# Attention with a gated convolution behind it: two narrow score blocks at a chunk's end are given one relu and one square in common

## The chip, the cores and the metric

One Trainium2 chip, of which one core is used. TensorE (PE in the profile) multiplies, VectorE (DVE) and ScalarE (ACT) work elementwise, GpSimd (POOL) does a little, and SyncE (SP) issues the transfers. The metric is the time of one launch on the device, in microseconds (us), as a median of several runs.

## The reference

For each of 8 batches of 3,200 rows, with `z` of 64 columns and `u`, `v` of 256:

```
scores = (1/3200) * z @ z.T               # 3200 x 3200
attn   = max(scores, 0) ** 2
x      = u * (attn @ v)
gate   = sigmoid(causal convolution of x, 5 taps, a weight per column and tap)
out    = ((x @ w_val) * gate) @ w_out
```

All is float32. The kernel reaches that precision by splitting a factor into a high and a low part, `hi = round(a)` and `lo = a - hi`, and by adding three products: low times high, high times low and high times high.

## The kernel before

The 3,200 keys of a batch are 25 tiles of 128 rows: 12 pairs of tiles and one single tile, 13 *blocks*. The queries are cut into 6 chunks of 4 tiles (512 columns), numbered 0 to 5, and one single tile that is done with chunk 5. A *step* is one block of keys for one chunk of queries, and a chunk runs through its 13 blocks at the *places* 0 to 12.

For a step TensorE first makes the scores `s` of the block (`scores`, L464), three steps ahead of use (`AHEAD`, L68). Then `weights_of` (L600) turns them into weights: on ScalarE a relu out of the accumulator banks into `a` (L643), a square in place (L644) and a copy to the high part `ah` (L646); on VectorE `al = a - ah` (L652). The attention `acc` (`attend`, L718) then multiplies `v`'s parts with `ah` and `al`. Its first product reads `ah`, its second `al`. TensorE runs two multiplications of 64 rows side by side, and each step's attention is in two parts, whose row halves change sides. The second part of a step waits in a list (`left`) until other work for TensorE comes up; that is mostly the scores of the step three ahead, which part the two parts of one step.

The scores are symmetric. What a chunk has computed is turned by VectorE (L518, L528), written to `mir` in memory by SP's queue and fetched as `m` by a later chunk (`mirrored`, L282), which then has no scores to compute there.

Two steps of a chunk are narrow. The single tile (`SINGLE`) has 512 scores for each row in place of 1,024. The second of the chunk's own two pairs (`own(c, 1)`) computes one half of its scores, 512 again, and takes the other from `m` (`halves`, L506; L608 to L628, with the relu at L611, the square at L612, and the two copies at L621). It is moved to the chunk's last place, L298. In the chunks in which no fetched block comes between, the single tile is at place 11 and this pair at place 12.

The work of the chunk behind (convolution, gate, the multiplication by `w_val`) is set out over the steps by tables (`BEHIND`, L328): at place 8 VectorE makes the second half of `gv` (`gate_value`, L912), at place 9 ScalarE copies it to `gvh` (`gate_value_high`, L916). In the loop over the steps (L1499) the order within a step is: TensorE's attention and scores, then the table's work (L1573), then `weights_of` for the step three ahead (L1579). Each engine takes its instructions in the order in which they are written.

The scores go to two bank pairs, `s0` and `s1`, in turn (`s_bank`, L455); each is 2 x 512 columns wide, and a narrow step uses 2 x 256 of it.

Of the kernel before, what the change touches and what calls it, by code (L numbers as in the profile page):

```python
# [7 lines left out]
F32 = mybir.dt.float32  # L8
# [4 lines left out]
P = 128  # L13
# [4 lines left out]
def attn_glu_kernel(  # L18
# [430 lines left out]

    st_, at = {}, {}  # L450

    next_s = [0]
    held_s = [None]

# [9 lines left out]
    def scores(b, c, i, terms=range(3)):  # L464
        if not terms:
            return
        k, n = tiles(c, i)
        w = sizes[c] * P
        if (b, c, i) not in st_:
            st_[b, c, i] = s_bank()  # L470
        s = st_[b, c, i]

        q = zt[b, c][:, :, :w].rearrange("p x (t a r) -> p x a t r", t=sizes[c], r=BLK)
        if has_copy(b, c, i):
            q = zq[b, c][:, :, :w].rearrange("p x (a y) -> p x a y", a=P // BLK)
        if halves(b, c, i):
            q, w = q[:, :, :, 2 * BLK :] if has_copy(b, c, i) else q[:, :, :, 2:], w // 2
        a = P // BLK
        sides = []
        for j in range(2):  # L480
            g, t = homes[k + (0 if n == 1 else j)]
            ks = slice(t * P, (t + 1) * P)
            qs = slice(j * (a // 2), (j + 1) * (a // 2)) if n == 1 else slice(0, a)
            kk = zt[b, g]
            mms = []
            for m in terms:
                kp, qp = (((0, 0), (0, 1), (1, 0)) if b == c == i == 0 else ((0, 1), (1, 0), (0, 0)))[m]
                mms.append((s[:, j, : w // 2 if n == 1 else w], kk[:, kp, ks], q[:, qp, qs], m == 0, m == 2))
            if both(c, i):
                for m in terms:  # L490
                    kp, qp = ((0, 1), (1, 0), (0, 0))[m]
                    q1 = zt[b, ONE][:, qp, j * (P // 2) : (j + 1) * (P // 2)]
                    mms.append((s[:, j, w // 2 : w // 2 + P // 2], kk[:, kp, ks], q1, m == 0, m == 2))
            sides.append(mms)
        side_by_side(*sides)
# [92 lines left out]
    def second_block(a, hi, lo, s):  # L588
        each = a.shape[1] // 2
        for j in range(2):  # L590
# [6 lines left out]
                v_low(0, 1)  # L597
            rest(lo[:, x], a[:, x], hi[:, x])

    def weights_of(b, c, i):  # L600

        k, n = tiles(c, i)
        w = sizes[c] * P
        ah = sb.tile([P, 2 * CW], F32R, name="ah", bufs=AHEAD + 1)
        al = sb.tile([P, 2 * CW], F32R, name="al", bufs=AHEAD + 1)
        cols = columns(c, i)
        hi, lo = ah[:, :cols], al[:, :cols]
        if halves(b, c, i):  # L608
            s = st_.pop((b, c, i))
            a = sb.tile([P, 2 * CW], F32, name="a", bufs=2)[:, :w]  # L610
            nc.scalar.activation(a.rearrange("p (j x) -> p j x", j=2), s[:, :, : w // 2], AF.Relu, scale=scale)  # L611
            nc.scalar.activation(a, a, AF.Square)  # L612
            m = m_in.pop((b, c, i))[:, :w]
            m = m.rearrange("p (a j x) -> p a j x", a=P // BLK, j=2)

            his, los = (x.rearrange("p (j a h x) -> p a j h x", j=2, a=P // BLK, h=2) for x in (hi, lo))
            a = a.rearrange("p (j a x) -> p j a x", j=2, a=P // BLK)
            parts = [(m, his[:, :, :, 0], los[:, :, :, 0])]
            parts.append((a, *(x[:, :, :, 1].rearrange("p a j x -> p j a x") for x in (his, los))))
            for src, h, _ in parts:  # L620
                nc.scalar.copy(h, src)  # L621
            at[b, c, i] = (ah, al)

            def rests():
                for src, h, l in parts:
                    nc.vector.tensor_tensor(l, src, f32(h), op=ALU.subtract)  # L626

            return rests  # L628
        if mirrored(b, c, i):
            a = m_in.pop((b, c, i))[:, :cols].rearrange("p (a j x) -> p a j x", a=P // BLK, j=n)  # L630
            hi, lo = (x.rearrange("p (j a x) -> p a j x", a=P // BLK, j=n) for x in (hi, lo))
        else:
            s = st_.pop((b, c, i))
            a = sb.tile([P, 2 * CW], F32, name="a", bufs=2)[:, :cols]
            each = n * w // 2
            if both(c, i):
                to = a[:, n * w :].rearrange("p (j x) -> p j x", j=2)
                nc.scalar.activation(to, s[:, :, each : each + P // 2], AF.Relu, scale=scale)
            if b == c == 0 and i < 2:
                at[b, c, i] = (ah, al)  # L640
                first_block(a, hi, lo, s) if i == 0 else second_block(a, hi, lo, s)
                return lambda: None
            nc.scalar.activation(a[:, : n * w].rearrange("p (j x) -> p j x", j=2), s[:, :, :each], AF.Relu, scale=scale)  # L643
            nc.scalar.activation(a, a, AF.Square)  # L644
        if cast_on_scalar(b, c, i):
            nc.scalar.copy(hi, a)  # L646
        else:
            nc.vector.tensor_copy(hi, a)
        at[b, c, i] = (ah, al)

        def rest():
            nc.vector.tensor_tensor(lo, a, f32(hi), op=ALU.subtract)  # L652
            if (b, c, i) == (0, 0, 2):
                v_high(b, 3)
                v_low(b, 3)
            if not mirrored(b, c, i):
                if c == 1 and two_pairs(b, c) and i == own(c, 0) and place[b, c, i] == 0:
                    return lambda: turn(b, c, i, a)
                turn(b, c, i, a)

        return rest
# [823 lines left out]
    with tc.manual_schedule():  # L1485
# [13 lines left out]
        for s in range(min(todo), END + 1):  # L1499
# [3 lines left out]
            late = steps[AHEAD - 1] if s == 0 else None  # L1503
            places, ends = (value_places(b, cm), project_places(b, cm)) if s >= 0 else ((), ())
            piece = PIECES[len(places)][places.index(p)] if p in places else None
            terms = [] if lacks(s) or not ahead else list(range(3))
            if s in FILL:
                no_wait(zeros[:, :P], zeros, "misc1", FILL[s])
            k = b * n_chunks + cm if s >= 0 else 0
# [4 lines left out]
            if s >= WHOLE_FROM:  # L1514
                assert not left and not terms and not piece and not before
                if s < END:
                    for h in range(DH):
                        attend_whole(b, c, i, h)
                        if s == WHOLE_FROM and h == 0:
                            one_turn(len(GROUPS) - 1)  # L1520
            else:
                fill, whole, bare = [], False, before and ends and not terms
                if before and ends:
                    project(*before, 0)
                    scores(*ahead, terms)
                    terms, fill = [], [(project, *before, 1, 0, len(ends) + 1)]
                elif before:
                    project(*before, 0)
                    scores(*ahead, terms[:1])
                    project(*before, 1)  # L1530
                    terms = terms[1:]
                if p in ends:
                    fill = [(project, *divmod(k - 2, n_chunks), 1, 1 + ends.index(p), len(ends) + 1)]
                if piece:
                    fill = [(value, *behind, *piece)]
                    behind = None
                fill += filling.get(s, [])
                if s >= NP and p == 0 and (bare or not before):

                    scores(*ahead, terms)  # L1540
                    for h in range(DH):
                        attend_whole(b, c, i, h)
                    terms, whole = (), True
                elif s >= 0 and c != ONE:
                    attend(b, c, i, 0)
                if late:
                    scores(*late)
                    attend(b, c, i, 1)
                    whole = True
                if s == -AHEAD:  # L1550
                    scores(*ahead, terms)
                    z_turn(0, 1)
                    terms = []
                if behind:
                    value(*behind, 0)
                if terms:
                    scores(*ahead, terms)
                for fn, *args in fill:
                    fn(*args)
                if s >= 0 and not whole and c != ONE:  # L1560
                    left.append((b, c, i))
                if terms or fill or behind or s + 1 == WHOLE_FROM:
                    for n in range(len(left)):
                        attend(*left.pop(0), 1, again=n > 0)
                if behind:
                    value(*behind, 1)
# [8 lines left out]
            keep()  # L1575
            if late:
                held.append(weights_of(*late))
            if ahead:
                held.append(weights_of(*ahead))  # L1579
                if s < 0 or s != ends_main[b, cm][1] - 1:  # L1580
                    for do in held[:]:
                        held.remove(do)
# [111 lines left out]
```

## Time and profile before

| | |
|---|---|
| median of 3 runs | 2251.35 us (2249.55 to 2252.07) |
| span of the profiled execution, first to last instruction | 2248.5 us |
| TensorE busy | 2241.3 us |
| VectorE busy | 1851.4 us |
| ScalarE busy | 1700.3 us |
| TensorE's granted clock over the span | 1.000 |

The profile is of one execution, and its own time is known by its span alone, 2.85 us under the median. Busy time is the union of an engine's instructions. Multiplications are pipelined and their ends are modelled, so one is judged by its start and by the start of the next. A row of a timeline that joins several instructions shows the first start, the whole stretch and the count.

### The profile page before, as it was taken

The page shows a single profiled execution, that of the slowest core. Times are in us where ns is not written, and L with a number is a line of the kernel's source. Part 1 is how long each engine was busy: PE and PEld are TensorE (multiplying, and loading weights), DVE is VectorE, ACT ScalarE, POOL GpSimd, SP SyncE. Part 2 cuts the span into 40 slices and gives each one's busy share as a digit, 9 for nine tenths or more (in the row PEclk, how much of TensorE's full clock was granted, in tenths as well). Part 3 has the DMA queues.
Part 4 walks back from the last instruction along what each step waited for, and adds up shares of the span by engine and source line. Part 5 has one row for each costly group of instructions (what it writes and reads, how often), then busy time and mean ns, then how long its engine had stood idle before and what let it go on. Part 6 is the DMA issues. An engine that isn't in the chain of part 4 may idle for free.

```text
span 2248.5 us, 49885 instructions
## 1 busy us (share of the span) xinstructions
PE 2241.3 (100%) x20235; PEld 1881.1 (84%) x20235; DVE 1851.4 (82%) x2284; ACT 1700.3 (76%) x2136; POOL 93.4 (4%) x134
## 2 busy tenths in 40 slices
PE   9999999999999999999999999999999999999999
PEld 7888888888888988888888898888888889888888
DVE  8888788877889778887888968888788887888777
ACT  8986688766887668876698766987669776697764
POOL 0200000000000000000000000000000000000001
PEclk9999999999999999999999999999999999999999
DMA  6558867888677886788677876778867778687663
GB/s 156 115 140 206 211 147 163 189 184 196 159 169 180 187 195 153 175 188 195 170 172 166 191 192 166 171 180 181 209 142 186 178 181 203 144 187 175 169 177 103
DMA packets 702423, 390.79 MB, mean 174 GB/s; under 512 B 410608, under 2 KB 635888, under 8 KB 702192
## 3 DMA queue, kind: packets, MB, share of 16 engines
q1 hardware_dynamic: 701376, 387.21, 73.0%
q8 instruction: 158, 2.59, 0.5%
q14 instruction: 73, 0.60, 0.1%
q10 hardware_dynamic: 816, 0.39, 0.1%
HBM read 213.92 MB, written 173.54 MB: 172 GB/s over the span
## 4 chain that ended last, share of the span: by engine, by line
PE 99%; DMA 0%; DVE 0%; ACT 0%; issue 0%
PE acc L426 72%; PE s L426 14%; PE misc L426 12%; PE acc L736 1%; PE misc L731 0%; PE acc L731 0%; DMA z_rows<-in_z_dram 0%; PE s L866 0%; PE misc L975 0%; PE misc L201 0%; PE s L1202 0%; PE acc L892 0%; PE s L892 0%; DVE al L652 0%; PE misc L1101 0%; ACT ah L646 0%
## 5 line engine op out<-in xcount | busy, mean ns | idle before, releaser
L426 PE MATMUL acc<-ah,v_hl 64*128 64x512 f32 x9408 | 1581.4, 387 | 0.1
L426 PEld LDWEIGHTS acc<-ah,v_hl 64*128 64x128 f32 x9408 | 920.8, 184 | 169.3 <-issue 0.9
L426 PE MATMUL acc<-al,v_hl 64*128 64x512 f32 x4704 | 948.0, 387 | 0.1
L426 PEld LDWEIGHTS acc<-al,v_hl 64*128 64x128 f32 x4704 | 468.5, 184 | 84.2 <-DVE al L652 1.4
L652 DVE TENSOR_TENSOR al<-a,ah 128x1024 fp32r<-128x1024 f32 x342 | 392.4, 1147 | 173.9 <-ACT ah L646 172.5
L643 ACT ACTIVATE a<-s 128x1024 f32<-128x1024 f32 x342 | 329.2, 962 | 131.2 <-PE s L426 115.8
L646 ACT CAST ah<-m 128x1024 fp32r<-128x1024 f32 x258 | 269.3, 1047 | 168.3 <-PE acc L426 95.0
L644 ACT ACTIVATE a<-a 128x1024 f32<-128x1024 f32 x342 | 343.5, 1004 | 10.9
L652 DVE TENSOR_TENSOR al<-m,ah 128x1024 fp32r<-128x1024 f32 x258 | 312.3, 1211 | 36.4 <-ACT ah L646 36.0
L646 ACT CAST ah<-a 128x1024 fp32r<-128x1024 f32 (+1 forms) x320 | 316.8, 990 | 10.1
L518 DVE STREAM_TRANSPOSE turned<-a 128x1024 f32<-128x1024 f32 (+1 forms) x282 | 323.2, 1146 | 0.0
L814 DVE SCALAR_TENSOR_TENSOR gate<-x,cw,gate 128x512 f32<-128x512 f32 (+1 forms) x392 | 285.0, 727 | 4.3 <-ACT gate L812 0.6
L426 PE MATMUL s<-zq,zhl 64*128 64x512 f32 (+1 forms) x1596 | 222.2, 377 | 0.0
L426 PEld LDWEIGHTS s<-zq,zhl 64*128 64x128 f32 x1596 | 152.2, 184 | 28.9
L766 DVE TENSOR_TENSOR x<-acc,ut 128x512 f32<-128x512 f32 (+1 forms) x96 | 61.4, 680 | 78.4 <-PE acc L426 65.8
L818 ACT ACTIVATE gate<-gate 128x512 f32<-128x512 f32 (+1 forms) x98 | 60.9, 622 | 63.6 <-DVE gate L814 63.4
L916 ACT CAST gvh<-gv 128x512 fp32r<-128x512 f32 x94 | 58.3, 620 | 47.9 <-DVE gv L912 47.0
L912 DVE TENSOR_TENSOR gv<-misc,gate 128x512 f32<-128x512 f32 x94 | 64.4, 685 | 21.3 <-PE misc L426 17.0
L426 PE MATMUL misc<-xh,w_val_lo 64*128 64x512 f32 x376 | 76.8, 386 | 0.0
L426 PE MATMUL misc<-xh,w_val_hi 64*128 64x512 f32 x376 | 76.8, 386 | 0.0
L426 PE MATMUL misc<-xl,w_val_hi 64*128 64x512 f32 x376 | 76.8, 386 | 0.0
L626 DVE TENSOR_TENSOR al<-m,ah 128x512 fp32r<-128x512 f32 x46 | 31.8, 692 | 52.7 <-ACT ah L621 52.7
(200 smaller groups left out, 2054.4 us busy)
## 6 DMA issues: line engine op xcount, KB each, us to landing
mir<-turned SPq DMA_DIRECT2D x468, 256.0 KB, 4.1
m<-mir SPq DMA_DIRECT2D x234, 512.0 KB, 5.0
u_raw<-in_u_dram SPq DMA_DIRECT2D x384, 64.0 KB, 3.6
mir<-turned SPq DMA_DIRECT2D x376, 64.0 KB, 2.5
m<-mir SPq DMA_DIRECT2D x94, 256.0 KB, 4.5
out_dram<-ob SPq DMA_DIRECT2D x152, 128.0 KB, 3.2
v_raws<-in_v_dram SPq DMA_DIRECT2D x100, 128.0 KB, 6.2
z_raw<-in_z_dram SPq DMA_DIRECT2D x180, 64.0 KB, 3.2
```

The source lines that it names most:

```text
L426: ins = nc.tensor.matmul(out_, st[r], mv[r], start=first, stop=last)
L518: nc.vector.transpose(into[:, t : t + m], a[:, j * w : (j + m) * w].rearrange("p (t m x) -> p t m x", t=m, x=BLK))
L626: nc.vector.tensor_tensor(l, src, f32(h), op=ALU.subtract)
L643: nc.scalar.activation(a[:, : n * w].rearrange("p (j x) -> p j x", j=2), s[:, :, :each], AF.Relu, scale=scale)
L644: nc.scalar.activation(a, a, AF.Square)
L646: nc.scalar.copy(hi, a)
L652: nc.vector.tensor_tensor(lo, a, f32(hi), op=ALU.subtract)
L766: nc.vector.tensor_tensor(x[:, h, HALO + cols.start : HALO + cols.stop], accs[b, c][h][:, cols] if with_ is None else with_, ut[b, c][:, h ...
L814: nc.vector.scalar_tensor_tensor(g, tap, cw[:, h, k : k + 1], g, op0=ALU.mult, op1=ALU.add)
L818: nc.scalar.activation(g, g, AF.Sigmoid)
L912: nc.vector.tensor_tensor(gv[:, :w], pvs[b, c][e][:, :w], gates[b, c][:, e, :w], op=ALU.mult)
L916: nc.scalar.copy(gvs[b, c][0][:, e, :w], gv_[b, c, e][:, :w])
```

## The change

In the chunks where the single tile and the second own pair stand next to each other, last in the chunk (`joint`), their scores go into one bank pair: the single tile's into the first 256 columns of each bank, the pair's into the last 256. The single tile's scores are no longer issued at their own step but one step later, directly ahead of the pair's (`waits`, `singles`). `weights_of` for the single tile moves to that later step too. There `joint_a` makes one relu and one square over all 1,024 columns; the copies to the high part and the subtractions stay apart, and read their half of the common `a`. This holds for 23 places: chunks 2 and 3 of batch 0, and chunks 0 to 2 of batches 1 to 7.

```diff
+    def joint(b, c, i):
+        if c >= n_chunks - 1 or not two_pairs(b, c):
+            return False
+        pair = (SINGLE, own(c, 1))
+        return i in pair and place[b, c, pair[1]] == place[b, c, pair[0]] + 1
...
         if (b, c, i) not in st_:
             st_[b, c, i] = s_bank()
+            if joint(b, c, i):
+                st_[b, c, own(c, 1)] = st_[b, c, i]
         s = st_[b, c, i]
+        if joint(b, c, i) and i != SINGLE:
+            s = s[:, :, CW // 2 :]
...
+    def joint_a(b, c):
+        s = st_.pop((b, c, SINGLE))
+        st_.pop((b, c, own(c, 1)))
+        a = sb.tile([P, 2 * CW], F32, name="a", bufs=2)
+        nc.scalar.activation(a.rearrange("p (j x) -> p j x", j=2), s, AF.Relu, scale=scale)
+        nc.scalar.activation(a, a, AF.Square)
+        both_a[b, c] = a.rearrange("p (j y x) -> p j y x", j=2, y=2)
+
+    def weights_of_single(b, c):
+        joint_a(b, c)
+        ah = sb.tile([P, 2 * CW], F32R, name="ah", bufs=AHEAD + 1)
+        al = sb.tile([P, 2 * CW], F32R, name="al", bufs=AHEAD + 1)
+        hi, lo = (x[:, :CW].rearrange("p (j x) -> p j x", j=2) for x in (ah, al))
+        a = both_a[b, c][:, :, 0]
+        nc.scalar.copy(hi, a)
+        at[b, c, SINGLE] = (ah, al)
+        def rest():
+            nc.vector.tensor_tensor(lo, a, f32(hi), op=ALU.subtract)
+            turned_[b, c, ONE] = sb.tile([P, 4 * CW], F32, name="turned", bufs=2)
+            into = turned_[b, c, ONE][:, :CW].rearrange("p (j y) -> p j y", j=2)
+            nc.vector.transpose(into, a)
+            to_keep.append((b, c, ONE))
+        return rest
...
+        if joint(b, c, i) and i == SINGLE:
+            return weights_of_single(b, c)
...
         if halves(b, c, i):
-            s = st_.pop((b, c, i))
-            a = sb.tile([P, 2 * CW], F32, name="a", bufs=2)[:, :w]
-            nc.scalar.activation(a.rearrange("p (j x) -> p j x", j=2), s[:, :, : w // 2], AF.Relu, scale=scale)
-            nc.scalar.activation(a, a, AF.Square)
+            if joint(b, c, i):
+                a = both_a.pop((b, c))[:, :, 1]
+            else:
...
-            terms = [] if lacks(s) or not ahead else list(range(3))
+            waits = ahead and joint(*ahead) and ahead[2] == SINGLE
+            terms = [] if lacks(s) or not ahead or waits else list(range(3))
+            if ahead and joint(*ahead) and not waits:
+                singles = steps[s + AHEAD - 1]
+            else:
+                singles = None
...
+                if singles:
+                    scores(*singles)
                 if terms:
                     scores(*ahead, terms)
...
+            if singles:
+                held.append(weights_of(*singles))
             if ahead:
-                held.append(weights_of(*ahead))
+                if not waits:
+                    held.append(weights_of(*ahead))
```

On ScalarE, at the end of chunk 0 of batch 2, before. `zq` are the next chunk's queries; the first relu that follows is the single tile's, the one behind `gvh` is the second own pair's:

```order
L818 ACTIVATE gate<-gate 128x512
L246 CAST zq<-zhl_6012 128x512 x2
L643 ACTIVATE a<-s_8499 128x512
L644 ACTIVATE a<-a 128x512
L646 CAST ah<-a 128x512
L916 CAST gvh<-gv 128x512
L611 ACTIVATE a<-s_8553 128x512
L612 ACTIVATE a<-a 128x512
L621 CAST ah<-m 128x4x2x64
L621 CAST ah<-a 128x8x64
```

The same stretch after the change, where L963 is the copy to `gvh` (L916 before), L618 and L619 are the joint relu and square, L629 is the single tile's copy, L668 (twice) the pair's:

```order
L865 ACTIVATE gate<-gate 128x512
L246 CAST zq<-zhl_5987 128x512 x2
L963 CAST gvh<-gv 128x512
L618 ACTIVATE a<-s_8499 128x1024
L619 ACTIVATE a<-a 128x1024
L629 CAST ah<-a 128x512
L668 CAST ah<-m 128x4x2x64
L668 CAST ah<-a 128x8x64
L690 ACTIVATE a<-s_8566 128x1024
```

The single tile's relu, square and copy have gone from ahead of `gvh` to behind it, and the pair's relu and square are joined with them.

On TensorE, the same place, before: the last two products of place 8's first part, the single tile's scores, and the first of place 8's second part:

```order
L426 MATMUL acc_8057<-ah,v_hl_8205 128x512
L426 MATMUL acc_8056<-ah,v_hl_8205 128x512
L426 MATMUL s_8499<-zhl_5807,zhl_7523 128x256 x6
L426 MATMUL acc_8056<-ah,v_hl_8205 128x512
L426 MATMUL acc_8057<-ah,v_hl_8205 128x512
```

And after: the last two products of place 9's first part, both blocks' scores, and the first of place 8's second part:

```order
L426 MATMUL acc_8031<-ah,v_hl_7913 128x512
L426 MATMUL acc_8032<-ah,v_hl_7913 128x512
L426 MATMUL s_8499<-zhl_5787,zhl_7498 128x256 x6
L426 MATMUL s_8499<-zhl_5787 128x256 x6
L426 MATMUL acc_8032<-ah,v_hl_8180 128x512
L426 MATMUL acc_8031<-ah,v_hl_8180 128x512
```

Place 9's first part (its `v` parts are `v_hl_7938` before and `v_hl_7913` after) now stands ahead of the single tile's scores and of place 8's second part. TensorE's further order, from the first product of place 10 on, has the same work ahead of it as before. VectorE's order is unchanged.

## Rows read from the trace of the kernel before

**Rows 1.** The page: busy time by engine; the chain that ended last, by engine.
```profile
PE 2241.3 (100%) x20235; PEld 1881.1 (84%) x20235; DVE 1851.4 (82%) x2284; ACT 1700.3 (76%) x2136; POOL 93.4 (4%) x134
...
PE 99%; DMA 0%; DVE 0%; ACT 0%; issue 0%
```

**Rows 2.** Table by line, whole span: shapes, count | busy, mean ns | idle before.
```profile
L426 PE MATMUL acc<-ah,v_hl 64*128 64x512 f32 x9408 | 1581.4, 387 | 0.1
```

**Rows 3.** Timeline, ScalarE, batch 2, chunk 0's end: start us, us, line, operation, [idle].
```profile
600.96 0.59 ACT L643 ACTIVATE a<-s 128x512 f32<-128x512 f32 x1
...
603.31 0.62 ACT L916 CAST gvh<-gv 128x512 fp32r<-128x512 f32 x1 [0.45 <-DVE gv L912]
603.84 0.59 ACT L611 ACTIVATE a<-s 128x512 f32<-128x512 f32 x1
...
605.51 0.62 ACT L621 CAST ah<-a 128x512 fp32r<-128x512 f32 x1
606.03 1.02 ACT L643 ACTIVATE a<-s 128x1024 f32<-128x1024 f32 x1
607.08 1.06 ACT L644 ACTIVATE a<-a 128x1024 f32<-128x1024 f32 x1
```

**Rows 4.** Timeline, VectorE, the same stretch.
```profile
600.67 1.24 DVE L518 STREAM_TRANSPOSE turned<-a 128x1024 f32<-128x1024 f32 x1
...
602.59 0.69 DVE L912 TENSOR_TENSOR gv<-misc,gate 128x512 f32<-128x512 f32 x1
603.19 0.68 DVE L652 TENSOR_TENSOR al<-a,ah 128x512 fp32r<-128x512 f32 x1
```

**Rows 5.** Timeline, TensorE, the same stretch.
```profile
600.81 0.52 PE L426 MATMUL s<-zhl 64*128 64x256 f32 x6
601.16 0.40 PE L426 MATMUL acc<-ah,v_hl 64*128 64x512 f32 x2
...
606.21 0.39 PE L426 MATMUL acc<-al,v_hl 64*128 64x512 f32 x2
606.43 0.39 PE L426 MATMUL acc<-ah,v_hl 64*128 64x512 f32 x2
...
608.25 0.39 PE L426 MATMUL acc<-al,v_hl 64*128 64x512 f32 x2
```

**Rows 6.** Timeline, all engines, batch 2, chunk 1's end.
```profile
649.31 0.59 ACT L611 ACTIVATE a<-s 128x512 f32<-128x512 f32 x1
...
652.53 0.39 PE L426 MATMUL acc<-al,v_hl 64*128 64x512 f32 x2
```

**Rows 7.** Timeline, all engines, batch 1, chunk 2's end.
```profile
416.67 0.69 DVE L912 TENSOR_TENSOR gv<-misc,gate 128x512 f32<-128x512 f32 x1
...
418.16 0.59 ACT L611 ACTIVATE a<-s 128x512 f32<-128x512 f32 x1
...
422.36 0.39 PE L426 MATMUL acc<-al,v_hl 64*128 64x512 f32 x2
```

**Rows 8.** Timeline, all engines, batch 2, chunk 2, places 8 and 9.
```profile
688.89 1.23 DVE L652 TENSOR_TENSOR al<-a,ah 128x1024 fp32r<-128x1024 f32 x1 [0.64 <-ACT ah L646]
...
691.66 0.39 PE L426 MATMUL acc<-al,v_hl 64*128 64x512 f32 x2
```

**Rows 9.** Timeline, all engines, batch 1, chunk 0's end.
```profile
328.71 0.59 ACT L611 ACTIVATE a<-s 128x512 f32<-128x512 f32 x1
...
330.38 0.39 PE L426 MATMUL acc<-al,v_hl 64*128 64x512 f32 x2
```

**Rows 10.** Timeline, all engines, batch 2, chunk 2, its first places.
```profile
666.46 1.23 DVE L652 TENSOR_TENSOR al<-a,ah 128x1024 fp32r<-128x1024 f32 x1 [1.10 <-ACT ah L646]
...
670.86 1.21 DVE L652 TENSOR_TENSOR al<-m,ah 128x1024 fp32r<-128x1024 f32 x1
...
672.12 0.50 PE L426 MATMUL acc<-al,v_hl 64*128 64x512 f32 x2
```

**Rows 11.** Who waited for whom, whole span: us in total, times, longest us.
```profile
ACT a L643 <- PE s L426: 115.8, 77, 4.6
```

More of the change, by code (lines that the diff above doesn't have):

```diff
@@ L598, in second_block @@
             rest(lo[:, x], a[:, x], hi[:, x])
+    both_a = {}
+    def joint_a(b, c):
[20 more added lines that the diff above has]
+        return rest
     def weights_of(b, c, i):
@@ L608, in weights_of @@
         if halves(b, c, i):
-            s = st_.pop((b, c, i))
-            a = sb.tile([P, 2 * CW], F32, name="a", bufs=2)[:, :w]
-            nc.scalar.activation(a.rearrange("p (j x) -> p j x", j=2), s[:, :, : w // 2], AF.Relu, scale=scale)
-            nc.scalar.activation(a, a, AF.Square)
+            if joint(b, c, i):
+                a = both_a.pop((b, c))[:, :, 1]
+            else:
+                s = st_.pop((b, c, i))
+                a = sb.tile([P, 2 * CW], F32, name="a", bufs=2)[:, :w]
+                nc.scalar.activation(a.rearrange("p (j x) -> p j x", j=2), s[:, :, : w // 2], AF.Relu, scale=scale)
+                nc.scalar.activation(a, a, AF.Square)
+                a = a.rearrange("p (j x) -> p j x", j=2)
             m = m_in.pop((b, c, i))[:, :w]
@@ L616, in weights_of @@
             his, los = (x.rearrange("p (j a h x) -> p a j h x", j=2, a=P // BLK, h=2) for x in (hi, lo))
-            a = a.rearrange("p (j a x) -> p j a x", j=2, a=P // BLK)
+            a = a.rearrange("p j (a x) -> p j a x", a=P // BLK)
             parts = [(m, his[:, :, :, 0], los[:, :, :, 0])]
```

## The prediction

> **What bounds the kernel now.** First the page's busy line and its chain of waits [rows 1]: TensorE is busy for 2241.3 of 2248.5 us, and 99% of the chain that ended last is TensorE's own work. Then the table by line [rows 2]: the 9,408 multiplications that read `ah` stood idle for 0.1 us in all. So nothing that only makes ScalarE or VectorE cheaper can show; all that TensorE does not spend on columns is 2248.5 - 2241.3 = 7.2 us, most of it at the start. What can show is a wait that is new. So I read, around one joint place, when the weights are made and when TensorE first reads them: the timelines of ScalarE, VectorE and TensorE at the end of chunk 0 of batch 2 [rows 3 to 5], then the same at chunks 1 and 2 and in batch 1 [rows 6 to 10]. There are 23 joint places: two in batch 0 (its chunks 2 and 3, where the two blocks also stand last and next to each other) and three in each of batches 1 to 7. The three of a batch differ in what stands around them, and they repeat from batch to batch; so one of each is worked out and multiplied.
>
> **What the change removes.** Two relus of 0.59 us (rows 600.96 and 603.84 of [rows 3]) become one of 1.02 us (row 606.03). Two narrow squares become one of 1.06 (row 607.08); I put their saving at the relus' 0.16 us, an estimate from those rows. ScalarE saves some 0.32 us at each place, 23 x 0.32 = 7.4 us in all. TensorE's columns, and what VectorE and the DMA queue issue, stay the same in number. SP's one moved item, the four writes of the single block's turned weights, is read only in the batch's last chunk. I cost all of this at nothing: TensorE does not wait for ScalarE's total, and what hides it is TensorE's column time.
>
> **What it moves, and the main term.** ScalarE takes its work in order. Today the single block's relu stands ahead of `gvh` (L916), the copy that belongs to the chunk behind; `gvh` waits 0.45 us for VectorE's `gv` [rows 3], and `gv` stands behind a transpose of 1.24 us (row 600.67) and a subtraction that fills the time between [rows 4]. The single block uses that time: its relu starts at 600.96, its low part is ready at 603.19 + 0.68 = 603.87, and TensorE reads it at 606.21 [rows 5]. After the change the joint relu stands behind `gvh`, and nothing that `gv` waits for has become earlier. So the joint relu starts where the second block's relu starts today, J = 603.84. From J: relu, start to start, 607.08 - 606.03 = 1.05; the square 1.06 and 0.03 of handing over (607.08 - 606.03 - 1.02) = 1.09; the narrow cast 0.62 (row 605.51); 0.03 to VectorE (603.28, the end of `gv`, to 603.31); the subtraction 0.68. The single block's low part is ready at J + 3.47 = 607.31. TensorE starts 0.05 us behind such an end (670.86 + 1.21 = 672.07 against 672.12, [rows 10]). Its work ahead of the block is the same as before, so it stands still for 607.31 + 0.05 - 606.21 = 1.15 us. The second block's low part then comes behind that subtraction, the block's transpose and two subtractions of its own, three starts at 0.60 (602.59 to 603.19) and 0.68 to the last end: J + 2.79 + 2.48 = 609.11, against 608.25 + 1.15 = 609.40: no second wait, though only by 0.29.
>
> The end of chunk 0 then costs 1.15 us in each of batches 2 to 7; in batch 1 TensorE is nearer [rows 9]: J = 328.71, 328.71 + 3.47 + 0.05 - 330.38 = 1.85. Together 1.85 + 6 x 1.15 = **8.75 us**.
>
> Chunk 1 [rows 6]: 649.31 + 3.47 + 0.05 - 652.53 = 0.30; seven times, **2.1 us**.
>
> Chunk 2 of batches 1, 3 and 5 [rows 7]: `gv` ends at 416.67 + 0.69 = 417.36; today `gvh` starts 603.84 - 603.31 = 0.53 ahead of J = 418.16, so at 417.63, held up by ScalarE's own queue; without the single block's three instructions ahead it starts 0.03 behind `gv`, at 417.39, and J is 417.92. The single block fits; the second block does not: TensorE goes straight from one to the other here. 417.92 + 5.27 + 0.05 - 422.36 = 0.88 us; three times, **2.6 us**.
>
> Chunk 2 of batches 2, 4 and 6 [rows 8]: another order counts. With the single block's scores moved, the halves of the attention that used to stand ahead of place 9 (two blocks of six pairs of multiplications, at 606.43 - 606.21 = 0.22 us each, and the single block's six narrow score multiplications, 601.16 - 600.81 = 0.35, both in [rows 5]) come after it: place 9 is wanted 12 x 0.22 + 0.35 = 3.0 us sooner. Its low part is ready at 688.89 + 1.23 = 690.12 and is read at 691.66 today; 690.12 + 0.05 - (691.66 - 3.0) = 1.5 us. What the joint block would have cost behind it is contained in this wait, since TensorE comes to it later by as much. Three times, **4.5 us**. Chunk 2 of batch 7 and batch 0's two places, by the same steps, I put at some 0.9 us together, an estimate with no row of its own.
>
> **What follows later.** The joint place ends later on ScalarE. The first relu of the next chunk starts today 606.03 - 603.84 = 2.19 us after J; after the change J + 1.05 + 1.09 + three casts at 0.52 (605.51 to 606.03) = J + 3.70. ScalarE is 1.5 us behind where it was. Where TensorE has just stood for as long, that is even. In chunk 1 TensorE loses only 0.30, so ScalarE runs 1.2 us late against it. In batches 2, 4 and 6 it gets no rest after this: VectorE idles 1.10 us for ScalarE at 666.46, and the low part that ends at 672.07 is read 0.05 us later, with no slack left [rows 10]. 3 x 1.2 = 3.6 us; in batch 7, with a little slack, some 0.8 (estimate, without a row). **4.4 us**. Elsewhere the blocks after the joint place are ready more than 1.2 us early.
>
> **The sum.** 8.75 + 2.1 + 2.6 + 4.5 + 0.9 + 4.4 = 23.3 us. The profiled execution's span is 2248.5, 2.85 us under the median of the runs, 2251.35; the waits come inside the span, so 2251.35 + 23.3 = 2274.6, 2275 in round numbers. Term by term the unknown is how exactly a hand-over of 0.03 to 0.05 us and overlaps of 0.1 us hold: 0.1 us each way at some 26 places is 2.6 us; and the 4.4 us may be absent or be doubled. The forecast's own range is 2268 to 2281.
>
> **What the skill says.** The rows of ScalarE show ScalarE's fixed share: 0.59 us for 512 elements and 1.02 for 1024, so 0.16 us do not depend on the size [rows 3]. The Trainium skill (ScalarE: Activation LUTs, What ACT_TABLE_LOAD costs) gives 186 ns plus 0.833 ns per element for an ACTIVATE with immediate scale, which speaks for joining; the rows agree within 0.03 us. It is a rule for an engine that is waited for; the second rival gives its result.
>
> **Rivals.** *Hidden, no change* (chance 0.08): the joint relu starts early enough. For chunk 0 it must start by 603.84 - 1.15 = 602.69, and `gv` end by 602.1. Against it: `gv` ends at 603.28 behind VectorE work that the change does not touch [rows 4]. For it: TensorE's reads may be placed later than the records say, since ends on TensorE are modelled. 2251.
>
> *Faster* (0.02): ScalarE's 7.4 us were being waited for somewhere. The bound is TensorE's whole idle time, 7.2 us [rows 1]: 2244 at best. Against it is the 0.1 us of [rows 2].
>
> *Direct waits at the joint blocks only* (0.08): neither place 9 nor the later block costs anything: 8.75 + 2.1 + 2.6 = 13.4, and 2265.
>
> *The lateness piles up* (0.10): at every place TensorE ends up waiting for ScalarE's full 1.5 us, whatever slack stands there now, because the next chunk's blocks are late too: 23 x 1.5 = 34.5, 2286. Against it: ScalarE's relus waited for TensorE's scores 77 times, 115.8 us in all [rows 11], and each such wait ends a lateness.
>
> That the change would not do what it says is out: the order of the built program shows the joint instructions behind `gvh`.
>
> **How the numbers follow.** The forecast has 0.72, the rivals 0.08, 0.02, 0.08 and 0.10. The range reaches down to the third rival less 3 us and up to the fourth: 2262 to 2286; outside lie the hidden and the faster case and a tail of the last. About 0.2% (4.5 us) is what a measurement of this kernel can tell from no change. Faster than that: 0.02. Within: 0.08. Slower: 0.90.
>
> **What would show it.** In the new profile ScalarE's joint relu should start within 0.1 us of the end of `gvh`, and VectorE should idle ahead of the single block's subtraction for some 3.3 us at the end of chunk 0 (from 603.28 to J + 2.79). TensorE should have a gap of about 1.1 us ahead of the first pair that reads the single block there, 0.3 in chunk 1, and in chunk 2 of even batches one ahead of place 9. The idle time ahead of the multiplications should rise from 0.1 to over 15 us in all, with `al` and `ah` as what ended it. If TensorE shows no such gaps the main term is wrong; if the gaps are there and grow from chunk to chunk, the fourth rival holds.

## The result, and the profile after

The changed kernel takes 2277.82 us (2277.16 to 2279.49 in 4 runs), the kernel before 2251.15 (2249.55 to 2252.07) beside it: a ratio of 1.012, interval 1.0108 to 1.0132. It is slower by 26.7 us; the prediction said 23.3, with 2275 for the time. The profiled executions differ by 2275.4 - 2248.5 = 26.9 us, so the profile holds the whole difference. The granted clock over the span is 1.000 in both.

The page after: its first line, the busy line and the chain by engine [rows 1], and from its table of the costliest groups (count | busy us, mean ns | idle us ahead of them, and what ended most of it) the multiplications of [rows 2] and the copy to `gvh`.

```profile
span 2275.4 us, 49860 instructions
...
PE 2251.5 (99%) x20235; PEld 1879.5 (83%) x20235; DVE 1849.8 (81%) x2284; ACT 1693.5 (74%) x2090; POOL 93.4 (4%) x134
...
PE 70%; ACT 11%; DVE 11%; issue 3%; DMA 3%; SPq 2%; DVEq 0%; ACTq 0%
...
L426 PE MATMUL acc<-ah,v_hl 64*128 64x512 f32 x9408 | 1580.0, 387 | 5.2 <-ACT ah L629 4.0
...
L426 PE MATMUL acc<-al,v_hl 64*128 64x512 f32 x4704 | 951.7, 388 | 11.9 <-DVE al L699 8.3
...
L963 ACT CAST gvh<-gv 128x512 fp32r<-128x512 f32 x94 | 58.3, 620 | 91.8 <-DVE gv L959 91.3
```

ScalarE's busy time fell by 1700.3 - 1693.5 = 6.8 us, as it was meant to. TensorE's multiplications, which waited for practically nothing before, now stand idle for 5.2 + 11.9 = 17.1 us, and the chain that ended last runs through ScalarE and VectorE for 22% of the span. The idle time is less than the 26.9 us lost, and TensorE's busy time rose by 10.2 us for the same 20,235 multiplications: a pair's record of 0.39 us reaches some 0.17 past the place where the next pair would start, and a pair that starts after a wait has a record of 0.50, so a part of each standstill is booked as work. The standstills below are therefore counted from start to start.

ScalarE at the end of chunk 0 of batch 2, the place of [rows 3] (start us, us, line, operation, idle before and what ended it):

```profile
607.77 0.62 ACT L963 CAST gvh<-gv 128x512 fp32r<-128x512 f32 x1 [2.26 <-DVE gv L959]
608.29 1.02 ACT L618 ACTIVATE a<-s 128x1024 f32<-128x1024 f32 x1
609.35 1.06 ACT L619 ACTIVATE a<-a 128x1024 f32<-128x1024 f32 x1
610.44 0.62 ACT L629 CAST ah<-a 128x512 fp32r<-128x512 f32 x1
```

VectorE there [rows 4]:

```profile
607.04 0.69 DVE L959 TENSOR_TENSOR gv<-misc,gate 128x512 f32<-128x512 f32 x1
611.09 0.69 DVE L633 TENSOR_TENSOR al<-a,ah 128x512 fp32r<-128x512 f32 x1 [3.35 <-ACT ah L629]
```

TensorE there [rows 5]:

```profile
610.19 0.39 PE L426 MATMUL acc<-ah,v_hl 64*128 64x512 f32 x2
611.11 0.50 PE L426 MATMUL acc<-ah,v_hl 64*128 64x512 f32 x2 [0.53 <-ACT ah L629]
611.83 0.50 PE L426 MATMUL acc<-al,v_hl 64*128 64x512 f32 x2 [0.22 <-DVE al L633]
612.17 0.40 PE L426 MATMUL acc<-ah,v_hl 64*128 64x512 f32 x2
```

The three timelines are read from top to bottom as one story. ScalarE has nothing to do for 2.26 us, because the next instruction in its order, `gvh`, waits for `gv`. Before, the single tile's relu, square and copy ran in a part of that time [rows 3]; now the joint relu comes 0.52 us behind the start of `gvh`. VectorE then idles for 3.35 us until it can make the single tile's `al`, and TensorE's two readers of that block come late. In a run of pairs 0.23 us apart the pair of 611.11 would have started at 610.42, so that wait costs 0.69; the pair of 611.83 would follow at 611.34, which costs 0.49; and the pair behind it comes 0.34 us later rather than 0.23, which costs 0.11. Together this place costs some 1.30 us.

The other kinds of place, on TensorE, in the order of the rows: places 9 and 12 of chunk 2 of batch 1 [rows 7]; the end of chunk 1 of batch 2 [rows 6]; place 4 of chunk 2 of the same batch, where the later wait was forecast [rows 10]; and place 9 of that chunk [rows 8].

```profile
415.92 0.50 PE L426 MATMUL acc<-al,v_hl 64*128 64x512 f32 x2 [0.51 <-DVE al L699]
...
426.69 0.50 PE L426 MATMUL acc<-al,v_hl 64*128 64x512 f32 x2 [0.25 <-DVE al L673]
...
658.66 0.50 PE L426 MATMUL acc<-al,v_hl 64*128 64x512 f32 x2 [0.19 <-DVE al L633]
...
679.45 0.50 PE L426 MATMUL acc<-al,v_hl 64*128 64x512 f32 x2 [1.13 <-DVE al L699]
679.79 0.62 PE L426 MATMUL acc<-ah,v_hl 64*128 64x512 f32 x4
...
696.22 0.51 PE L426 MATMUL acc<-ah,v_hl 64*128 64x512 f32 x2 [0.39 <-ACT ah L693]
...
697.48 0.50 PE L426 MATMUL acc<-al,v_hl 64*128 64x512 f32 x2 [0.75 <-DVE al L699]
```

Going through all such rows of the trace, from start to start and against the same rows before, the time lost comes to:

| where | forecast, us | measured, us |
|---|---|---|
| chunk 0, b1 and b2 to b7 | 1.85 + 6 x 1.15 = 8.75 | 2.01 + 6 x 1.30 to 1.33: 9.90 |
| chunk 1, b1 to b7 | 7 x 0.30 = 2.1 | 0.43 to 0.51 each: 3.19 |
| chunk 2 of b1, b3, b5 | 3 x 0.88 = 2.6 | 1.29, 1.25, 1.29: 3.83 |
| chunk 2 of b2, b4, b6 | 3 x 1.5 = 4.5 | 1.56, 1.52, 1.51: 4.59 |
| place 4 of chunk 2 in b2, b4, b6 and b7 | 4.4 | 1.09, 1.06, 1.11, 0.86: 4.12 |
| b0's two places, chunk 2 of b7 | 0.9 | 0.26, 0.47, 0.53: 1.26 |
| sum | 23.3 | 26.9 |

The sum is the difference of the two spans, so there is no other loss to look for.

### The profile page after: what moved, and what is told of

Its sections match the earlier page's. It is cut to its first block, busy times and chain, and to the rows that moved or that the text cites. A ratio compares the mean times of both kernels' runs of the same rounds, so it can differ in the third digit from the quotient of the medians.

```text
span 2275.4 us, 49860 instructions
## 1 busy us (share of the span) xinstructions
PE 2251.5 (99%) x20235; PEld 1879.5 (83%) x20235; DVE 1849.8 (81%) x2284; ACT 1693.5 (74%) x2090; POOL 93.4 (4%) x134
## 4 chain that ended last, share of the span: by engine, by line
PE 70%; ACT 11%; DVE 11%; issue 3%; DMA 3%; SPq 2%; DVEq 0%; ACTq 0%
PE acc L426 49%; PE s L426 10%; PE misc L426 9%; DVE al L699 3%; ACT a L691 3%; DVE turned L529 3%; ACT a L690 3%; ACT ah L693 2%; DMA mir<-turned 1%; PE acc L783 1%; DVE gate L861 1%; SPq L555 1%; SPq L161 1%; DMA u_raw<-in_u_dram 1%; ACT gvh L963 1%
## 5 line engine op out<-in xcount | busy, mean ns | idle before, releaser
L426 PE MATMUL acc<-al,v_hl 64*128 64x512 f32 x4704 | 951.7, 388 | 11.9 <-DVE al L699 8.3
L699 DVE TENSOR_TENSOR al<-a,ah 128x1024 fp32r<-128x1024 f32 (+2 forms) x319 | 376.5, 1180 | 161.4 <-ACT ah L693 160.3
L690 ACT ACTIVATE a<-s 128x1024 f32<-128x1024 f32 (+1 forms) x319 | 315.5, 989 | 123.3 <-PE s L426 108.6
L691 ACT ACTIVATE a<-a 128x1024 f32<-128x1024 f32 (+2 forms) x319 | 328.9, 1031 | 10.1
L693 ACT CAST ah<-a 128x1024 fp32r<-128x1024 f32 (+2 forms) x297 | 302.5, 1019 | 9.4
L529 DVE STREAM_TRANSPOSE turned<-a 128x1024 f32<-128x1024 f32 (+1 forms) x259 | 307.1, 1186 | 0.0
L963 ACT CAST gvh<-gv 128x512 fp32r<-128x512 f32 x94 | 58.3, 620 | 91.8 <-DVE gv L959 91.3
L633 DVE TENSOR_TENSOR al<-a,ah 128x512 fp32r<-128x512 f32 x23 | 15.9, 693 | 77.0 <-ACT ah L629 77.0
```

What stands on the lines that cost most here:

```text
L426: ins = nc.tensor.matmul(out_, st[r], mv[r], start=first, stop=last)
L529: nc.vector.transpose(into[:, t : t + m], a[:, j * w : (j + m) * w].rearrange("p (t m x) -> p t m x", t=m, x=BLK))
L963: nc.scalar.copy(gvs[b, c][0][:, e, :w], gv_[b, c, e][:, :w])
```

## The experiments

The theory: what costs is the place of the single tile's work in ScalarE's order, behind `gvh`, and beside it the moved scores (place 9). Its rivals: that it is the joining itself (the second block needs no relu of its own, but the first waits for a relu and a square of twice the length), that TensorE's new order is the cause of all of it, and that the losses add to each other from chunk to chunk. Each ratio is to the kernel before, measured beside it on the same chip, with a median of 2251.59 us (`early`, the split and the two with row halves turned) or 2250.85 (the others). Two parts of the change can be set apart: where `weights_of` for the single tile stands (ahead of the table's work, with `gvh` in it, or behind), and at which step its scores are issued.

### Joint instructions ahead of gvh

```diff
+            early = weights_of(*singles) if singles else None
             for fn, args in todo.get(s, ()):
                 fn(*args)
...
             if singles:
-                held.append(weights_of(*singles))
+                held.append(early)
```

> The changed kernel, but the joint relu, square and the single tile's copy are written ahead of the step's table work, so ahead of gvh on ScalarE. My theory (in-order wait behind gvh): the joint relu no longer starts behind gvh but when ScalarE reaches it, some 2.9 us sooner at the end of chunk 0; the waits at places 11 and 12 and the later ones in chunk 2 of batches 2, 4, 6, 7 go. What stays is the wait at place 9, which comes from TensorE's order: 3 x 1.5 (chunk 2, even batches), 3 x 0.45 (odd batches), some 0.4 three times elsewhere: 7 us, 2258 us, 1.003 of before. Rival (the wide relu and square are themselves too long for the two steps left): place 11 still waits, about 2270 or more. Rival (shared bank pair or scores issued later cost on TensorE): about 2278 as before this edit.

Measured: 2256.16 us (2255.31 to 2256.69), ratio 1.002, interval 1.001 to 1.0029. ScalarE at the end of chunk 0 of batch 2 in this kernel:

```profile
603.16 1.02 ACT L618 ACTIVATE a<-s 128x1024 f32<-128x1024 f32 x1
604.21 1.06 ACT L619 ACTIVATE a<-a 128x1024 f32<-128x1024 f32 x1
605.31 0.62 ACT L629 CAST ah<-a 128x512 fp32r<-128x512 f32 x1
605.83 0.62 ACT L963 CAST gvh<-gv 128x512 fp32r<-128x512 f32 x1
```

`gvh` no longer waits for `gv`: the joint work fills that time. All waits at places 11 and 12 and the later ones at place 4 are gone, and 22.1 of the 26.7 us with them (2256.16 - 2251.59 = 4.6 are left), by moving one call by a few lines. What is left is place 9; on TensorE in chunk 2 of batch 2:

```profile
690.56 0.50 PE L426 MATMUL acc<-ah,v_hl 64*128 64x512 f32 x2 [0.33 <-ACT ah L693]
...
691.82 0.50 PE L426 MATMUL acc<-al,v_hl 64*128 64x512 f32 x2 [0.76 <-DVE al L699]
```

That is some 1.65 us in each of batches 2, 4 and 6. Batches 1, 3 and 5 lose 0.53 each at place 9 as well, which the prediction had not seen: it had put this wait in the even batches alone. Batch 7, batch 0 and chunk 0 of batch 1 lose some 0.4 to 0.5 each. These losses are more than the 4.6 us, because some 0.75 us comes back in each of batches 2, 4 and 6: 0.30 at place 4 of chunk 2, where TensorE no longer makes the small stop that it makes before (672.12 [rows 10]), and 0.45 in the blocks behind that chunk.

### The scores at their old step, joint instructions ahead of gvh

```diff
-            terms = [] if lacks(s) or not ahead or waits else list(range(3))
+            terms = [] if lacks(s) or not ahead else list(range(3))
...
-                if singles:
-                    scores(*singles)
```

This comes on top of the edit above. TensorE's order is then the kernel before's; the joint relu and square are all that is new.

> The changed kernel, but the single tile's scores stay at their old step (TensorE's order is that of the kernel before), and the joint relu, square and copy are written ahead of the step's table work, so ahead of gvh. Theory: no wait is left, and no turn of row halves is added as in the run with the flushed second parts; 2251.5 us, ratio 0.999 to 1.001, though ScalarE has some 7 us less to do. Rival (sharing the bank pair, or the wide relu, costs something by itself): above 2255. Rival (ScalarE's saving is time once nothing waits): below 2247.

Measured: 2252.34 us (2250.78 to 2253.72, 11 runs) against 2250.85, ratio 1.0006, interval 0.9997 to 1.0015: no difference clear of noise. The busy line of this kernel's page, ScalarE at the same place, and TensorE at place 4 of chunk 2 of batch 2:

```profile
PE 2241.5 (100%) x20235; PEld 1882.5 (84%) x20235; DVE 1851.7 (82%) x2284; ACT 1693.8 (75%) x2090; POOL 91.2 (4%) x134
```

```profile
602.57 1.03 ACT L618 ACTIVATE a<-s 128x1024 f32<-128x1024 f32 x1 [0.31 <-PE s L426]
...
605.25 0.62 ACT L963 CAST gvh<-gv 128x512 fp32r<-128x512 f32 x1
```

```profile
673.75 0.50 PE L426 MATMUL acc<-al,v_hl 64*128 64x512 f32 x2 [0.46 <-DVE al L699]
```

The joint relu now waits 0.31 us for the second block's scores, which is the price of joining as such. The expectation that no wait is left was not quite met: place 4 of chunk 2 of batches 2, 4 and 6, where TensorE had no slack, waits 0.46 us. But from start to start TensorE gets 0.43 of it back in the blocks behind that chunk, so nothing is left of it in the time. ScalarE is busy 1700.3 - 1693.8 = 6.5 us less than before and the time is no shorter: the saving is real and buys nothing, since TensorE waited for none of it. This is the fastest of these versions with a joint relu, and it does not beat the kernel before. It also settles the rival that the joining itself is what costs.

### The scores at their old step, joint instructions behind gvh

The edit to `terms` and `singles` of the last section, without `early`: the other half of the two by two.

> The changed kernel, but the single tile's scores stay at their old step, with TensorE's order that of the kernel before; the joint relu stays behind gvh. Theory: the waits at place 9 go, all those behind gvh stay: 8.95 in chunk 0, 2.45 in chunk 1, 6.7 in chunk 2, 0.4 in batch 0 and 4.45 later: 23 us, 2274.5 us. Rival (the order of TensorE is the main cause): about 2255.

Measured: 2277.53 us (2277.3 to 2278.82), ratio 1.012, interval 1.0106 to 1.0134. That is the changed kernel's time, with TensorE's order unchanged; 2274.5 was expected. TensorE at the end of chunk 0 of batch 2:

```profile
612.13 0.51 PE L426 MATMUL acc<-ah,v_hl 64*128 64x512 f32 x2 [0.86 <-ACT ah L629]
612.86 0.51 PE L426 MATMUL acc<-al,v_hl 64*128 64x512 f32 x2 [0.22 <-DVE al L633]
```

In batches 3 to 7 the first of these waits is 0.50 to 0.52; why it is 0.86 in batch 2 is open. The waits at place 9 are gone, but the ones behind the joint block then come in full in chunk 2, which loses 1.32 us in each of the odd batches and 1.52 to 1.56 in the even ones: 8.6 us in all, where 6.7 was expected. So place 9's waits did not add to the others; they stood in their place. The position behind `gvh` is by itself enough for the whole loss. With the scores moved as well, the same lateness is only met two or three places sooner. The four kernels side by side, each less the kernel before that was measured beside it, in us:

| | scores at their old step | scores moved |
|---|---|---|
| joint relu ahead of `gvh` | 2252.34 - 2250.85 = 1.5 | 2256.16 - 2251.59 = 4.6 |
| joint relu behind `gvh` | 2277.53 - 2250.85 = 26.7 | 2277.82 - 2251.15 = 26.7 |

The first row against the second is 25.2 and 22.1 us; the first column against the second 3.1 and nothing.

### One chunk alone

The joint places limited to one chunk of batches 1 to 7, by a list that `joint` looks into; all else as in the changed kernel.

```diff
+    ONLY = [(b, 0) for b in range(1, B)]
...
-        if c >= n_chunks - 1 or not two_pairs(b, c):
+        if c >= n_chunks - 1 or not two_pairs(b, c) or (b, c) not in ONLY:
```

> The change at chunk 0 of batches 1 to 7 alone. Theory: 1.18 us at place 11 in six batches and 1.87 in batch 1, with nothing later: 8.95 us, 2260.4. Rival (the lateness is carried on from place to place): with the other places left alone it would still show at later blocks, above 2264.

> The change at chunk 1 of batches 1 to 7 alone. Theory: each of the seven waits 0.35 us at place 11, and ScalarE comes 1.2 us late to the next chunk, which costs 1.2 us at place 4 of chunk 2 in batches 2, 4, 6 and 0.85 in batch 7: 2.45 + 4.45 = 6.9 us, 2258.4. Rival (the wait in chunk 2 belongs to other joint places, so each place costs its own wait alone): 2.45, 2254.

Measured: chunk 0 alone 2260.93 us (2260.29 to 2262.12), ratio 1.0046, interval 1.0032 to 1.0059; chunk 1 alone (with `(b, 1)` in the list) 2258.0 (2256.93 to 2258.58), ratio 1.0031, interval 1.0019 to 1.0043. Chunk 0 loses 2.00 us at its end in batch 1, 1.25 to 1.32 in batches 2, 3, 5, 6 and 7 and 1.55 in batch 4, and nothing later. Chunk 1 alone has its small wait at the joint block, and then place 4 of the next chunk; both in batch 2, on TensorE:

```profile
653.37 0.50 PE L426 MATMUL acc<-al,v_hl 64*128 64x512 f32 x2 [0.20 <-DVE al L635]
...
674.15 0.50 PE L426 MATMUL acc<-al,v_hl 64*128 64x512 f32 x2 [1.09 <-DVE al L701]
```

The later wait of 1.1 us is thus chunk 1's: it is there without any joint place in chunk 0 or 2, and it is absent with chunk 0's alone. It comes some 20 us after its cause, at a line that the change does not touch. The two losses, 10.1 and 7.2 us, are those of the same places in the changed kernel (9.9, and 3.2 + 4.1), where all chunks are joined. That settles the rival by which lateness piles up from chunk to chunk.

### Two relus and two squares again, both behind gvh

The scores still share a bank pair and are still moved, but each block has a relu and a square of its own.

```diff
-        nc.scalar.activation(a.rearrange("p (j x) -> p j x", j=2), s, AF.Relu, scale=scale)
-        nc.scalar.activation(a, a, AF.Square)
...
+        half_a(b, c, s, 0)
+        both_s[b, c] = s
...
+    def half_a(b, c, s, y):
+        to = both_a[b, c][:, :, y]
+        nc.scalar.activation(to, s.rearrange("p j (y x) -> p j y x", y=2)[:, :, y], AF.Relu, scale=scale)
+        nc.scalar.activation(to, to, AF.Square)
...
+                half_a(b, c, both_s.pop((b, c)), 1)
```

> The changed kernel with one thing undone: relu and square are two narrow ones again, the single tile's first, then its copy, then the pair's, all still behind gvh and out of the shared bank pair. Theory (place behind gvh first, width second): the single tile's low part comes at J + 2.62 in place of J + 3.47, so chunk 0 waits 0.30 in place of 1.18 six times and about 1.0 in batch 1, chunk 1 not at all; place 9 keeps its 1.68 x 3, 0.88 x 3 and 1.2 in all elsewhere; ScalarE comes 1.8 us late in place of 1.5 to the next chunk, so the later waits grow to about 6.9. Sum 18.6, about 2270 us. Rival (width is the cause): about 2255. Rival (width has no part): about 2278.

Measured: 2276.64 us (2276.08 to 2277.77), ratio 1.0113, interval 1.0098 to 1.0128; 2270 was expected. The joint place did become cheaper, as expected: 0.35 us at place 11 of chunk 0, 0.70 to 0.75 with what follows up to place 12, and nothing in chunk 1. But behind chunk 1's joint place ScalarE is later against TensorE, by the 0.32 us that joining saves and by the 0.45 us that TensorE no longer loses there, and the wait at place 4 of chunk 2 in batches 2, 4 and 6 grows by as much, from 1.1 to 1.87 us. TensorE there in batch 2, and its stretches around it (from:to, us, busy us (instructions), granted clock, DMA share, GB/s):

```profile
679.89 0.50 PE L426 MATMUL acc<-al,v_hl 64*128 64x512 f32 x2 [1.88 <-DVE al L707]
...
681.62 1.48 PE L426 MATMUL s<-zq,zhl 64*128 64x512 f32 x6
```

```profile
677.00:680.00 3.00, 1.12 (x12) 1.00 0.77 180
680.00:681.00 1.00, 1.00 (x8) 0.79 0.80 264
681.00:684.00 3.00, 3.00 (x16) 0.50 0.64 106
684.00:687.00 3.00, 3.00 (x28) 1.00 0.93 161
```

After the standstill TensorE was granted 0.50, its level of 1.2 GHz, for some 3.4 us: the six score multiplications take 1.48 us where they take 0.84 otherwise. That costs 1.60 to 1.63 us at each of the three places on top of the wait, and all four runs show it: their granted clock over the span is 0.997 to 0.999. The expectation had the longer waits (6.9 us in all), but not the clock, 4.8 of the 6.6 us by which it missed; nor had it place 4 of chunk 2 in batches 1, 3 and 5, which now loses 0.60 each. Against the rival "the joining itself" this run says little: without the clock's part it would stand some 6 us below the changed kernel (an estimate, 2276.64 - 3 x 1.6 against 2277.82), so the wide relu has a part in the loss behind `gvh`, but most of the loss is there with nothing joined.

### The turn of row halves ahead of the scores

To take place 9's wait away, the second part of place 8's attention is issued at its old step, although no scores come there:

```diff
-                if terms or fill or behind or s + 1 == WHOLE_FROM:
+                if terms or fill or behind or waits or s + 1 == WHOLE_FROM:
```

> The changed kernel, but the second parts of the attention that the single tile's scores used to part from place 9 are issued at their old step, so place 9 is wanted no sooner than in the kernel before. Theory: the waits at place 9 go (they measured 0.3 to 1.6 us in nine places), those behind gvh stay: 8.95 in chunk 0, 2.45 in chunk 1, 3.4 and 3.3 in chunk 2, 0.4 in batch 0, 4.45 later on: 23 us, 2274 us; up to 2.3 more if the turn of row halves with nothing between costs 0.1 us in each of 23 places. Rival (TensorE's order is the main cause): about 2255.

> Both edits on the changed kernel: the joint relu ahead of gvh, and TensorE's second parts at their old step. Theory: nothing of the 26.7 us is left; 2251 us, or up to 2253 if each turn of row halves costs 0.1 us; ratio 0.999 to 1.001. ScalarE's saving of some 7 us buys nothing. Rival (sharing a bank pair, or scores one step later, costs by itself): above 2256. Rival (ScalarE's saving is worth time once the waits are gone): below 2247.

Measured: 2278.88 us (2278.06 to 2280.28), ratio 1.0124, interval 1.0107 to 1.0141, with this alone; 2261.18 (2259.33 to 2261.51), ratio 1.0042, interval 1.0027 to 1.0057, with `early` too. Both miss, and in the same way. The waits at place 9 go, but at each of the 23 places TensorE now turns from one part to the other with nothing between. TensorE in batch 2's chunk 0, in the kernel with this edit alone:

```profile
602.20 0.39 PE L426 MATMUL acc<-al,v_hl 64*128 64x512 f32 x2
602.42 0.95 PE L426 MATMUL acc<-ah,v_hl 64*128 64x512 f32 x4
603.21 0.40 PE L426 MATMUL acc<-al,v_hl 64*128 64x512 f32 x2
603.45 0.63 PE L426 MATMUL acc<-ah,v_hl 64*128 64x512 f32 x4
603.92 0.39 PE L426 MATMUL acc<-al,v_hl 64*128 64x512 f32 x2
```

From the row of 602.42 to the next, two pairs, it is 0.79 us; from 603.45 to the next, two pairs as well, 0.47. Over the 0.45 that two pairs take in most rows, a turn costs 0.34 us, and I had allowed 0.1. The trace has the second pair of the row of 602.42 start at 602.88, 0.23 later than in an unbroken run of pairs; by the trace's semaphores it waits for an earlier product of TensorE's own. The other 0.11 is what follows a pair that had waited. For `early_flush`, 23 x 0.34 = 7.8 us is most of the 8 to 10 us by which it missed. Some 2 us more are lost around chunks 4 and 5 of batch 0 in its profile. There VectorE waits 2.25 us for an output transfer at 228.19 (1.27 in the kernel before) and ScalarE 5.24 us for a fetched block at 240.48 (3.82 before); why these transfers come later is open.

## Why the prediction was right

**What bounds the kernel.** It held: TensorE's time is the time, and ScalarE's total is not. 6.5 us less of it brought nothing where hardly a wait was made (2252.34). With that the second rival, *faster*, falls. The fixed share of an instruction was saved: 6.8 us over the 2136 - 2090 = 46 instructions that ScalarE has fewer, 0.15 each. The time does not follow this saving. The Trainium skill (ScalarE: Activation LUTs, What ACT_TABLE_LOAD costs) gives 186 ns for this share and 0.833 ns per element, by which the joint relu would take 1.04 us, an estimate from that page; the row has 1.02.

**The main term.** It held in mechanism and nearly in size. The joint relu starts at 608.29, within 0.1 us of the end of `gvh` (607.77 + 0.62 = 608.39). VectorE's idle time ahead of the single tile's subtraction was forecast at 3.3 us and is 3.35. TensorE's gap in chunk 0, forecast at 1.15 us, is 0.69 + 0.49 = 1.18, though in two parts, one ahead of each of the block's two readers, and not all ahead of the first pair. That the second block needs no wait of its own there held too. Ahead versus behind `gvh` at unchanged TensorE order (2252.34 against 2277.53) shows that this place in the order is the cause.

**The term that was mis-sized** is the one that I left at nothing: what TensorE loses in getting going again. Behind a pair that had waited, the next starts 0.34 us later rather than 0.23 (611.83 to 612.17, 679.45 to 679.79). It could have been read in the trace before: the low part read at 672.12 [rows 10] is such a pair, and its record of 0.50 us says that something is different there. It explains 1.30 for 1.15, and most of 0.43 to 0.51 for 0.30. At the 17 places of chunk 0, chunk 1 and the odd batches' chunk 2 it is 1.9 us, more than half of the 3.6 us by which the sum fell short.

**Chunk 2 of the odd batches** was the step that failed in its working, though for little. The prediction's J is 417.92. In the new trace the joint relu starts at 421.35, and TensorE, ahead of place 9, is 3.18 us behind its time in the trace of before, so J is 418.17 by that clock: 0.25 us later, because ScalarE and VectorE come to this place that much later against TensorE. ScalarE there:

```profile
420.82 0.62 ACT L963 CAST gvh<-gv 128x512 fp32r<-128x512 f32 x1 [1.47 <-DVE gv L959]
421.35 1.02 ACT L618 ACTIVATE a<-s 128x1024 f32<-128x1024 f32 x1
```

With 0.11 for getting going again that makes 0.88 + 0.25 + 0.11 = 1.24, and the odd batches lose 1.25 to 1.29 us. More than half of it falls at place 9 (415.92), which the prediction had excluded for them.

**Chunk 2 of the even batches** and **the later wait** came out within 0.3 us in sum (4.59 for 4.5, 4.12 for 4.4). That is closer than the working deserves, for getting going again is missing there too. At place 4 the shorter wait answers what chunk 1 lost more: of ScalarE's 1.5 us, 0.45 rather than 0.30 is taken up there, which leaves 1.05. The statement that place 9's wait contains the joint block's was tested by keeping the scores where they were: the time stayed, as it should. The runs with chunk 0 and chunk 1 alone put the later wait where the prediction had it.

**The rivals.** *Hidden* falls by the gaps on TensorE. *Direct waits only*, 2265, falls by place 4 and place 9. *The lateness piles up* falls by the three later waits of 1.09, 1.06 and 1.11 us, which do not grow, and by chunk 0, behind which nothing is late.

## What to carry to other kernels

Joining two instructions of an engine that nobody waits for saves nothing, and it moves the first one's work to where the second stands. Before such an edit, look in that engine's timeline at what stands between the two: if there is an instruction in it that waits for another engine, the earlier piece was using that wait, and behind it the piece becomes late by the whole of it. And price the restart of a stalled TensorE as well as its gap, and look for the follow-up of a lateness in the next stage that has no slack, even at lines that the edit doesn't touch.

## What the hardware showed that I had not expected

- A pair of attention multiplications that had waited is followed 0.34 us later rather than 0.23: 0.11 us for each standstill, whether the wait ahead of it was 0.2 or 1.1 us.
- A turn from one part of the attention to the other, with the row halves changed and no scores between, costs 0.34 us: the first pair starts 0.23 late, and the same 0.11 follows it.
- After a standstill of 1.88 to 1.91 us TensorE went to a granted 0.50 for some 3.4 us, three times in the run with the instructions split. After the 1.37 us at the same place of batch 7 in that run, and after the 1.13 us in the changed kernel, it did not. TensorE in the changed kernel, in the stretches that answer to those above:

```profile
679.40:680.40 1.00, 0.95 (x8) 1.00 0.81 268
680.40:683.40 3.00, 3.00 (x30) 1.00 0.58 95
```

TensorE in the split run, behind the 1.37 us of batch 7:

```profile
2089.95:2091.00 1.05, 1.05 (x8) 1.00 0.86 301
2091.00:2094.00 3.00, 3.00 (x30) 1.00 0.67 120
```
